# Sliding-window attention block with MLP on one core: Q and K as token rows transposed by DMA, V once per token, one-bank PSUM tiles

## The chip, the cores and the metric

The program runs on one core of a Trainium2 chip. The metric is the device time of the whole program in microseconds; three runs of the kernel before gave 184.72, 181.6 and 182.56 us, median 182.56 us. Engine names are those of the profile: PE is TensorE (PEld its weight loads), DVE is VectorE, ACT is ScalarE, POOL is GpSimd, and SP is SyncE, the queue from which nearly every DMA is issued. L12 is line 12 of the kernel file that is spoken of.

## What is computed

One transformer block on 2048 tokens of width 448 (16 heads of 28), all tensors bf16. A vector `c` gives six modulation rows. Attention is local and dilated: each token looks at itself and the 7 tokens at distance 2, 4, ... 14 before it.

```python
sa, ca, ga, sb, cb, gb = split(silu(c) @ w_mod, 6)
h = layernorm(x) * (1 + ca) + sa
q, k, v = heads(h @ wqkv)                       # 16 heads of 28
logits = q[s] . k[s - 2*w] * 28**-0.5           # w = 0..7, masked where s - 2*w < 0
x = x + ga * (softmax(logits) @ v) @ wo
h = layernorm(x) * (1 + cb) + sb
x = x + gb * (gelu(layernorm(h) @ w1 + b1) @ w2 + b2)     # 448 -> 1792 -> 448
```

## The kernel before, in words

**Layout.** The tokens are split by parity `s` (the dilation is 2, so a window is 8 neighbours of one parity) and into eight blocks `jb` of 2 x 128 tokens. The list of steps in `ORDER` (L32) is the program: each name is a method of the class, and each engine runs its instructions in the order in which the list issues them. `SLOTS` (L68) gives each step its buffer. Nothing is reordered later.

**Norm and transpose.** `s1`, `r1` and `n1` normalise a block. Blocks 0 to 3 are transposed on PE (`tr`, L385) and moved out of PSUM with the modulation applied (`ev`, L392, half on DVE and half on ACT). Blocks 4 to 7 are transposed by DMA from SP (`dT`, L402) and then modulated on DVE (`sc`, L407). The result is `hT`, channels on partitions, with 16 columns of zeros ahead.

**Q and K.** Each of the 16 heads is padded from 28 to 32 columns: `wc` (L441) spreads the weights, and `qk` (L448) computes four pieces of 256 padded channels, with weights stationary and tokens moving, for the groups of blocks 0, 1, 2+3, 4+5, 6+7. The result has channels on partitions, as the logits need it, and `qe` (L467) copies it to `qT` and `kT` on ACT. A piece is an accumulation in two halves, `first` (L415, eight matmuls) and `second` (L422, six matmuls): pairs of 64-row matmuls share the array, and the second half swaps the row halves. Between the halves stands `ob` (L432), a nop on SP, ACT, POOL or DVE that waits for the first half; the second half waits for the nop. So a nop that stands in a queue behind something slow holds PE up.

**V and the attention step.** The attention runs in nine steps `i` of 2 x 57 queries per parity. `v_` (L480) computes V anew for the 64 keys of each of the four windows of a step, 28 matmuls of 64 x 64 x 448 per step, and `ve` (L503) copies it on ACT. `L` (L512) makes the logits, 64 matmuls of 57 columns; `eA` and `eB` (L526) exponentiate them on ACT; `mA` and `mB` (L537) mask them on DVE; `AV` (L548) makes the sums and the outputs; `ln` (L567) and `rx` (L571) make 1/sum on ACT; `mu` (L575) multiplies on DVE. `wo` (L583) and `x1` (L591) project and add the residual.

**The MLP.** `s2` to `n3` norm and modulate, `dY` (L627) transposes by DMA, `f1` (L631, again in halves), `ge` (L652) and `f2` (L656) run over four chunks of 512 tokens, `fo` (L663) adds and `dS` stores. The last three attention steps lie among the MLP's first two chunks.

**PSUM.** Four tiles of two banks each (L97). One ACT or DVE instruction empties both banks: 896 to 1024 columns for Q, K, V, the logits, the sums, `x1` and most of `fo`.

**The row broadcast.** `rowm` (L301) makes four modulation rows on PE, `rowc` copies them, `dR` (L313) writes them to DRAM, and `dR2` (L316) reads them back to all partitions. Both are issued on SP, and `dR2` waits for `dR`.

Of the kernel before, what the change touches and what calls it, by code (L numbers as in the profile page):

```python
# [36 lines left out]
qA.0.1 ob.POOL.q.0.0 ob.ACT.q.1.2 n1.2 r1.3 qB.0.0 ob.ACT.q.0.1 qB.1.2 qe.0.0 tr.2 n1.3 qe.1.2 rowm ev.2.3 ev.2.2
ev.2.0 ev.2.1 tr.3 rowc qB.0.1 ev.3.2 ev.3.1 qA.0.2 ev.3.0 ev.3.3 s1.6 qA.1.1 ob.SP.q.0.2 qe.0.1 qB.0.2 ob.SP.q.1.1
qA.2.2 qe.0.2 dR s1.5 r1.6 qB.1.1 ob.SP.q.2.2 L.0 qe.1.1 s1.4 r1.5 qB.2.2 eA.0 dB qA.2.1 eB.0 mA.0 r1.4 qA.1.0 s1.7
ob.SP.q.2.1 qe.2.2 qB.2.1 ob.SP.q.1.0 qB.1.0 qe.2.1 qA.2.0 mB.0 r1.7 n1.4 dR2 qe.1.0 AV.0 ob.POOL.q.2.0 n1.5 dT.4  # L40
n1.6 qB.2.0 ln.0 qA.1.3 rx.0 dT.6 b1T ob.DVE.q.1.3 b1c qB.1.3 qe.2.0 mu.0 vA.1 dT.5 qe.1.3 vA.2 ob.POOL.v.1 wos vB.1
# [20 lines left out]
r2.7 n2.7 h2.7 f2.3.1 s3.7 r3.7 f2.5.0 n3.7 fo.3 dY.7 xp.6 dS.3 f2.5.1 fA.3.0 fo.5 fA.3.1 ob.SP.f.3.0 xp.7 dS.5
fB.3.0 ob.SP.f.3.1 fB.3.1 ge.3.0 fA.3.2 ge.3.1 ge.3.3 fA.3.3 ob.SP.f.3.2 ge.3.2 fB.3.2 ob.SP.f.3.3 fA.3.4 ge.3.5
ge.3.4 fB.3.3 ob.SP.f.3.4 fA.3.5 ge.3.6 ge.3.7 fB.3.4 ob.SP.f.3.5 fA.3.6 ge.3.9 ge.3.8 fB.3.5 ob.SP.f.3.6 fB.3.6
ge.3.11 f2.4.1 ge.3.10 ge.3.12 ge.3.13 f2.6.0 fo.4 dS.4 f2.6.1 f2.7.0 fo.6 dS.6 f2.7.1 fo.7.0 dS.7.0 fo.7.1 dS.7.1
"""
# [675 lines left out]
```

## Time and profile before

| | before |
|---|---|
| median of three runs | 182.56 us (181.6 to 184.72) |
| the profiled execution: span from the first to the last instruction | 182.2 us (the page gives no other time of it) |
| PE busy | 170.8 us, 2538 matmuls |
| DVE, ACT, POOL busy | 112.5, 105.0, 43.3 us |
| DMA | 15.51 MB, 21455 packets |
| mean granted TensorE clock | 0.958 |

The page gives busy time by engine, then 40 equal slices of the span (4.56 us each) in tenths of busy time, then the chain of work that ended last and the costliest groups. A group of the costliest instructions reads: line, engine, operation, output <- input, shape, count | busy us, mean ns of one | idle time before it and what ended it. A row of the windows table gives busy time, with the number of instructions in brackets, in one stretch of the span.

### The profile page before, as it was taken

What the parts mean: (1) busy time and instruction counts of PE and PEld (TensorE: products, weight loads), DVE (VectorE), ACT (ScalarE), POOL (GpSimd) and SP (SyncE); (2) the same over time, 40 slices, a digit from 0 to 9 for tenths busy, and PEclk for the clock granted to TensorE, in tenths of its full rate; (3) what the DMA queues carried; (4) which work ended last, traced back from release to release, by engine and by line L of the source; (5) the groups of instructions that cost most, each with busy time, mean ns of one, the idle gap of its engine ahead of it and who ended that gap; (6) DMA issues with size and microseconds to landing.
All of it is one profiled execution on the core that took longest, in us unless ns stands there. A gap on an engine that the chain in (4) does not pass through costs nothing.

```text
span 182.2 us, 5815 instructions
## 1 busy us (share of the span) xinstructions
PE 170.8 (94%) x2538; PEld 86.3 (47%) x2539; DVE 112.5 (62%) x264; ACT 105.0 (58%) x145; POOL 43.3 (24%) x77
## 2 busy tenths in 40 slices
PE   7999679979999979999999999999999999999990
PEld 2556335634444453444454554554544554454550
DVE  5858757599969789589788604785970772002022
ACT  3177619777967497487884879650887000585000
POOL 7404062000050442062402500224520224400000
PEclk9969969999999995899999999999999999999998
DMA  5999994997000300300080130013103004100111
GB/s 150 321 393 302 375 312 101 117 255 153 4 4 2 61 4 4 63 0 5 0 105 14 56 58 4 4 24 84 54 4 58 0 0 108 54 0 0 54 50 50
DMA packets 21455, 15.51 MB, mean 85 GB/s; under 512 B 13301, under 2 KB 20982, under 8 KB 21430
## 3 DMA queue, kind: packets, MB, share of 16 engines
q1 hardware_dynamic: 21428, 15.14, 32.1%
q8 instruction: 20, 0.33, 0.8%
q14 instruction: 5, 0.04, 0.1%
q10 hardware_dynamic: 2, 0.00, 0.0%
HBM read 10.04 MB, written 1.95 MB: 66 GB/s over the span
## 4 chain that ended last, share of the span: by engine, by line
PE 74%; DMA 8%; DVE 7%; ACT 4%; issue 2%; SPq 1%; POOL 1%; DVEq 0%
PE P L660 21%; PE P L419 18%; PE P L428 13%; PE P L588 7%; PE P L489 7%; DMA rowd<-zt 3%; DMA bc<-rowd 3%; DMA yT<-in_w_mod_dram 2%; PE P L563 2%; DVE st L348 2%; PE P L522 1%; PE P L554 1%; PE P L261 1%; PE P L292 1%; ACT et L527 1%
## 5 line engine op out<-in xcount | busy, mean ns | idle before, releaser
L653 ACT ACTIVATE hm<-P,b1c 128x512 bf16<-128x512 f32 x56 | 34.1, 691 | 22.4 <-PE P L428 22.3
L660 PE MATMUL P<-w2s,hm 128*128 128x448 bf16 x224 | 43.4, 353 | 0.0
L660 PEld LDWEIGHTS <-hm 128*128 128x128 bf16 x224 | 21.6, 98 | 20.6 <-issue 0.8
L419 PE MATMUL P<-yT,w1s 64*128 64x512 bf16 x224 | 27.1, 376 | 0.2 <-DVE x L665 0.2
L597 POOL TENSOR_TENSOR xp<-x,gbb 128x896 f32<-128x896 bf16 x8 | 15.2, 1897 | 40.2 <-DVE x L593 27.7
L665 DVE TENSOR_TENSOR x<-P,xp 128x896 bf16<-128x896 f32 (+1 forms) x9 | 8.8, 985 | 25.8 <-PE P L660 25.7
L354 POOL TENSOR_SCALAR rs<-mv 128x2 f32<-128x2 f32 x22 | 6.7, 303 | 70.8 <-DVE mv L350 61.8
L428 PE MATMUL P<-yT,w1s 64*128 64x512 bf16 x168 | 20.9, 376 | 0.0
L348 DVE BATCH_NORM_STATS2 st<-x 128x6 f32<-128x448 bf16 x32 | 18.3, 615 | 0.9 <-DMA x<-in_A_x_dram 0.5
L489 PE MATMUL P<-wv,hT 64*64 64x448 bf16 x252 | 17.5, 397 | 0.4 <-SPq L437 0.2
L593 DVE TENSOR_TENSOR x<-P,x 128x896 bf16<-128x896 f32 x8 | 8.7, 1090 | 14.5 <-PE P L588 14.5
L419 PEld LDWEIGHTS <-w1s 64*128 64x128 bf16 x224 | 11.1, 94 | 13.0 <-issue 1.2
L527 ACT ACTIVATE et<-P 128x912 bf16<-128x912 f32 x18 | 16.1, 942 | 1.7 <-PE P L522 1.7
L419 PE MATMUL P<-hT,wqk 64*128 64x512 bf16 (+1 forms) x160 | 16.9, 347 | 0.1
L428 PE MATMUL P<-hT,wqk 64*128 64x512 bf16 (+1 forms) x120 | 13.6, 349 | 3.6 <-SPq L437 3.6
L355 POOL TENSOR_TENSOR rs<-rs,nhalf 128x2 f32<-128x2 f32 x22 | 16.0, 726 | 1.8
L568 ACT ACTIVATE rc<-P 128x912 f32<-128x912 f32 x9 | 8.5, 942 | 10.4 <-PE P L554 10.4
L540 DVE TENSOR_TENSOR et<-et,mask 128x912 bf16<-128x912 bf16 x18 | 11.3, 652 | 4.5 <-ACT et L527 4.4
L588 PE MATMUL P<-wo,qT 128*128 128x448 bf16 x64 | 13.5, 353 | 0.1
L428 PEld LDWEIGHTS <-w1s 64*128 64x128 bf16 x168 | 8.8, 94 | 9.4
L578 DVE TENSOR_TENSOR qT<-P,rc 128x456 bf16<-128x456 f32 x18 | 10.5, 624 | 2.9 <-ACT rc L573 2.9
L509 ACT CAST vs<-P 128x896 bf16<-128x896 f32 x9 | 8.1, 907 | 6.2 <-PE P L489 6.2
(79 smaller groups left out, 187.2 us busy)
## 6 DMA issues: line engine op xcount, KB each, us to landing
w1s<-in_B_w_dram SPq DMA_DIRECT2D x4, 448.0 KB, 11.7
w2s<-in_B_w_dram SPq DMA_DIRECT2D x2, 784.0 KB, 15.6
out_dram<-x SPq DMA_DIRECT2D x7, 224.0 KB, 2.3
hm<-in_w_mod_dram SPq DMA_DIRECT2D x1, 1344.0 KB
hm<-in_A_wqkv_dram SPq DMA_DIRECT2D x4, 224.0 KB, 5.1
x<-in_A_x_dram SPq DMA_DIRECT2D x1, 896.0 KB
yT<-in_w_mod_dram SPq DMA_DIRECT2D x3, 224.0 KB, 4.1
x<-in_A_x_dram SPq DMA_DIRECT2D x2, 224.0 KB
```

Source lines behind the costliest of these rows:

```text
L348: nc.vector.bn_stats(out=self.st[:, b + s, :], in_=src[:, s, :])
L355: nc.gpsimd.tensor_tensor(out=r, in0=r, in1=self.nhalf[:], op=ALU.pow)
L419: mm = self.nc.tensor.matmul(outs[t], lhsT=lhs(t, r, kt), rhs=rhs(t, r, kt), start=(kt == 0), stop=False)
L428: mm = self.nc.tensor.matmul(outs[o], lhsT=lhs(o, r, kt), rhs=rhs(o, r, kt), start=False, stop=(n == 2))
L489: mm = self.nc.tensor.matmul(t[64 * s:64 * s + 64, o, 0:D], lhsT=self.hT[r, s, kt, k0:k0 + NK], rhs=self.wv[r, kt, :], start=(part == 0 an ...
L527: self.nc.scalar.activation(out=self.et[:, self.sl(f"e{i}"), 2 * h:2 * h + 2, :], in_=self.ps(f"L{'AB'[h]}{i}")[:, :, 0:8 * NQ], func=ACT.Exp,
L540: self.nc.vector.tensor_tensor(out=e, in0=e, in1=m, op=ALU.mult)
L578: self.nc.vector.tensor_tensor(out=self.qT[:, s, :, c0:c0 + SW], in0=self.ps(f"O{i}")[:, s, 0:8 * NQ].rearrange("p (m c) -> p m c", m=4), ...
L588: self.nc.tensor.matmul(p[:, s, 0:D], lhsT=self.qT[:, s, m, c0:c0 + 128], rhs=self.wo[:, m, :], start=(m == 0), stop=(m == 3))
L597: self.nc.gpsimd.tensor_tensor(out=self.xp[:, self.sl(f"xp{jb}"), :, :], in0=self.x[:, jb, :, :], in1=self.gbb2[:].unsqueeze(1).to_broadca ...
L653: self.nc.scalar.activation(out=self.hid(c)[:, ft, :], in_=self.ps(f"F{c}.{ft // 2}")[:, ft % 2, :], func=ACT.Gelu_apprx_tanh, bias=self.b ...
L660: self.nc.tensor.matmul(p[:, s, 0:D], lhsT=h[:, ft, 128 * b:128 * b + 128], rhs=self.w2s[:, ft, :], start=(ft == 0), stop=(ft == FT - 1))
```

## The change

- **Q and K with tokens as rows.** `qk` takes the token block as the stationary operand (128 tokens) and the weights, unpadded, as the moving one: 448 columns of Q into one bank and 448 of K into another, for each block and parity. `wc` is gone; the weights are used as they come from DRAM. Each bank is copied to a staging tile `qks` with the heads spread to 32 columns (`qe`, on ACT or DVE, one bank each), and a DMA transpose from SP (`qT`) turns the 128 x 1024 staging tile into the transposed layout `qkT`. There are 16 such transposes.
- **V once per token.** `v` is computed as Q and K are, 14 matmuls per block. `ve` copies it to `vst`, `vw` writes it to a scratch tensor `vd` in DRAM, and `vr` reads the overlapping windows back, two per step. `dZ` writes the zero rows at the ends.
- **PSUM** is eight tiles of one bank, and every instruction that empties PSUM works on one bank: `ex`, `ln`, `rx`, `mu`, `x1`, `fo`.
- **Transposes of h.** Blocks 2 to 7 by DMA; only blocks 0 and 1 on PE. `sc` is one instruction per piece, on DVE or ACT.
- The modulation columns (`mod`) are made one slab of weights at a time, `wqk` and `wv` share the memory of the hidden layer, and `ORDER` and `SLOTS` are new throughout. The rest of the MLP's arithmetic is as before.

```diff
-        self.P = [ps.tile([128, 2, 512], FP32, name=f"P{i}") for i in range(4)]
+        self.P = [ps.tile([128, 512], FP32, name=f"P{i}") for i in range(8)]
...
-            return self.wqk[r, kt, 128 * (2 * p + o):128 * (2 * p + o) + 128]
+            return self.hT[r, s, kt, 128 * jb:128 * jb + 128]
...
-            return self.hT[r, :, kt, c0:c0 + 128 * nj]
-        return [t[:, 0, 0:n], t[:, 1, 0:n]], lhs, rhs
+            return self.wqk[r, kt, D * o:D * o + D]
+        return [p[:, 0:D] for p in self.ps(f"Q{jb}_{s}")], lhs, rhs
...
+    def qe(self, eng, jb, s, o):
+        out = self.qks[:, self.sl(f"q{jb}_{s}"), o, :].rearrange("p (h e) -> p h e", e=32)[:, :, 0:DH]
+        self.copy(eng, out, self.ps(f"Q{jb}_{s}")[o][:, 0:D].rearrange("p (h e) -> p h e", e=DH))
+
+    def qT(self, jb, s):
+        c0 = PADL + 128 * jb
+        src = self.qks[:, self.sl(f"q{jb}_{s}"), :, :].rearrange("p o n -> p (o n)")
+        self.nc.sync.dma_start_transpose(out=self.qkT[:, s, :, c0:c0 + 128], in_=src)
+
+    def v(self, jb):
+        def lhs(o, r, kt):
+            return self.hT[r, o, kt, 128 * jb:128 * jb + 128]
+
+        def rhs(o, r, kt):
+            return self.wv[r, kt, :]
+        return [p[:, 0:D] for p in self.ps(f"V{jb}")], lhs, rhs
+
+    def vw(self, jb):
+        a = WIN - 1 + 128 * jb
+        self.nc.sync.dma_start(out=self.vd[:, a:a + 128, :].rearrange("s r d -> r s d"),
+                               in_=self.vst[:, self.sl(f"vw{jb}"), :, :])
+
+    def vr(self, i, s):
+        src = self.vd[s, SW * i:SW * i + NK, :]
+        src = bass.AP(src.tensor, src.offset, [list(src.ap[0]), [NQ * D, 2], [1, D]])
+        self.nc.sync.dma_start(out=self.vs[64 * s:64 * s + 64, self.sl(f"v{i}"), :, 0:D], in_=src)
...
-        self.nc.scalar.activation(out=self.et[:, self.sl(f"e{i}"), 2 * h:2 * h + 2, :],
-                                  in_=self.ps(f"L{'AB'[h]}{i}")[:, :, 0:8 * NQ], func=ACT.Exp,
+    def ex(self, i, r):
+        self.nc.scalar.activation(out=self.et[:, self.sl(f"e{i}"), r, :], in_=self.ps(f"L{i}")[r][:, 0:8 * NQ],
...
-            if jb < 4:
+            if jb < NTR:
...
+NACT = 2
+NTR = 2
```

Three places of the new order matter to the prediction. The first is the start of ACT's queue, with what each instruction waits for (hT<-P is `ev`, hT<-hT is `sc`; DMAHW names the semaphore of a DMA; wqk<-hm is `wc`). Before:

```order
L400 ACTIVATE hT<-P_65,mcol 128x2x128 x2
L446 COPY wqk<-hm 128x512 x2
L400 ACTIVATE hT<-P_66,mcol 128x2x128 x2
L446 COPY wqk<-hm 128x512
L509 CAST vs<-P_64 128x2x448
L478 CAST kT<-P_63 128x2x2x128
```

The change, up to the first copy of Q and the first of V:

```order
L416 ACTIVATE hT<-P_65,mcol 128x2x128 [waits DVE_49,PE_49]
L416 ACTIVATE hT<-P_67,mcol 128x2x128 [waits DVE_49,PE_49]
L416 ACTIVATE hT<-hT,mcol 128x2x128 [waits DMAHW5_49]
L416 ACTIVATE hT<-hT,mcol 128x2x128
L475 CAST qks<-P_68 128x16x28 [waits PE_49]
L475 CAST qks<-P_70 128x16x28 [waits PE_49]
L475 CAST vst<-P_63 128x448 [waits PE_49]
```

The weight copies are gone, and two `sc` of block 2, which wait for that block's DMA transpose, now stand ahead of the first copy of Q; the nop `ob.A.Q0_0`, for which the second half of the first Q and K piece waits on PE, stands in this queue right behind them.

The second place is ACT from the last copies of Q and K ahead of the first logits (`L.0`) on. Before:

```order
L478 CAST qT<-P_65 128x2x2x128
L527 ACTIVATE et<-P_64 128x912
L527 ACTIVATE et<-P_63 128x912
L478 CAST kT<-P_66 128x2x2x256
L478 CAST qT<-P_65 128x2x2x256
L478 CAST qT<-P_64 128x2x2x128
L568 ACTIVATE rc<-P_65 128x912
L573 ACTIVATE rc<-rc 128x912
```

The change:

```order
L475 CAST qks<-P_70 128x16x28
L531 ACTIVATE et<-P_67 128x456
L531 ACTIVATE et<-P_66 128x456
L531 ACTIVATE et<-P_63 128x456
L531 ACTIVATE et<-P_65 128x456
L475 CAST qks<-P_68 128x16x28
L475 CAST qks<-P_69 128x16x28
L475 CAST qks<-P_64 128x16x28
L475 CAST vst<-P_67 128x448
L475 CAST vst<-P_66 128x448
```

One step's exponentials were two instructions of 912 columns and are four of 456; the first `ln` moved back behind the exponentials of two more steps.

The third place is SP around the row broadcast (rowd is `dR`, bc is `dR2`). Before:

```order
L187 DMA wo<-in_A_wo_dram 28x4x448 x4
L314 DMA rowd<-zt 128x448
L191 DMA b1r<-in_B_b_dram 14x128
L192 DMA b2bc<-in_B_b_dram 128x448
L318 DMA bc<-rowd 128x4x448
L405 DMA_TRANSPOSE hT<-yz 128x8x128 x3
```

The change:

```order
L424 DMA_TRANSPOSE hT<-yz 128x8x128
L512 DMA vs<-vd 64x2x448
L332 DMA rowd<-rows 128x448
L484 DMA_TRANSPOSE qkT<-qks 128x8x128
L206 DMA wo<-in_A_wo_dram 28x4x448
L336 DMA bc<-rowd 128x4x448
L484 DMA_TRANSPOSE qkT<-qks 128x8x128
L512 DMA vs<-vd 64x2x448
```

SP now also issues the transposes of Q and K and the reads of V, and the second transpose of block 3 stands behind `dR2`.

More of the change, by code (lines that the diff above doesn't have):

```diff
@@ L37 @@
[L37 to L41, printed above, removed]
@@ L62 @@
[L62 to L65, printed above, removed]
+i.mask i.z i.eps warm.3.4 i.one dX.0.1 dC cT warm.0.5 s1.0 silu0 silu1 warm.2.4 i.maskc r1.0 n1.0 i.ones dM.0 dX.2.2
@@ L288, in mod, with silu2 @@
+    def silu2(self):
+        self.nc.vector.tensor_copy(out=self.silub[:], in_=self.silu[:].unsqueeze(2).to_broadcast([128, 4, 32]))
+    def mod(self, kt):
+        p, r = self.ps("mod"), slice(0, min(128, D - 128 * kt))
         for v in range(2):
             for j in range(4):
-                for kt in range(4):
-                    r = slice(0, min(128, D - 128 * kt))
-                    self.nc.tensor.matmul(p[:, 1, 4 * v + j:4 * v + j + 1],
-                                          lhsT=self.wm1[r, kt, v * D + KO[j]:v * D + KO[j] + 128],
-                                          rhs=self.silu[r, kt:kt + 1], start=(kt == 0), stop=(kt == 3))
+                n = 8 * kt + 4 * v + j
+                self.nc.tensor.matmul(p[:, n:n + 1], lhsT=self.wm1[r, kt, v * D + KO[j]:v * D + KO[j] + 128],
+                                      rhs=self.silu[r, kt:kt + 1], start=True, stop=True)
@@ L310, in rowc @@
     def rowc(self):
-        self.nc.scalar.copy(out=self.rows, in_=self.ps("R")[:, 0, 0:D])
+        self.nc.scalar.copy(out=self.rows[:], in_=self.ps("R")[:, 0:D])
     def dR(self):
-        self.nc.sync.dma_start(out=self.rowd[:], in_=self.rows)
+        self.nc.sync.dma_start(out=self.rowd[:], in_=self.rows[:])
     def dR2(self):
@@ L478, in qe @@
             self.nc.scalar.copy(out=out, in_=src)
-    def v_(self, i, part):
-        t = self.ps(f"V{i}")
-        for n in range(4 if part == 0 else 3):
-            for row in range(2):
-                o = row if part == 0 else 1 - row
-                kt = n if part == 0 else REST[o][n]
-                k0 = PADL + SW * i + NQ * o - (WIN - 1)
-                r = slice(64 * row, 64 * row + 64)
-                for s in range(2):
-                    mm = self.nc.tensor.matmul(t[64 * s:64 * s + 64, o, 0:D], lhsT=self.hT[r, s, kt, k0:k0 + NK],
-                                               rhs=self.wv[r, kt, :], start=(part == 0 and n == 0),
-                                               stop=(part == 1 and n == 2), tile_position=(64 * row, 64 * s))
-                    if part == 1 and n == 0:
-                        self.tc.add_manual_dep(mm.ins, self.half[f"V{i}"], SYNC, reason="half")
-        if part == 0:
-            self.half[f"V{i}"] = mm
@@ L640, in rhs @@
             return y[r, :, kt, :]
-        return [t[:, 0, :], t[:, 1, :]], lhs, rhs
+        return [t[:, :] for t in self.ps(f"F{c}_{p}")], lhs, rhs
     def fA(self, c, p):
-        self.first(f"F{c}.{p}", *self.f1(c, p))
+        self.first(f"F{c}_{p}", *self.f1(c, p))
     def fB(self, c, p):
-        self.second(f"F{c}.{p}", *self.f1(c, p))
+        self.second(f"F{c}_{p}", *self.f1(c, p))
     def hid(self, c):
@@ L681, in emit @@
             name, args = "i_" + args[0], []
-        name = {"silu": "silu_", "w2s": "w2s_", "b1c": "b1c_", "wo": "wo_", "xp": "xp_"}.get(name, name)
-        getattr(self, name)(*[int(a) for a in args])
-WC_DVE = {(0, 0), (0, 2), (1, 0), (1, 2)}
-QE_DVE = set()
-VE_DVE = set()
+        name = {"w2s": "w2s_", "b1c": "b1c_", "wo": "wo_", "xp": "xp_"}.get(name, name)
+        getattr(self, name)(*[int(a) if a.isdigit() else a for a in args])
+NACT = 2
+NTR = 2
 @with_exitstack
```

347 lines of the change are left out of this document (162 added, 185 removed).

## The prediction, made before the changed kernel ran

> **What bounds the kernel now.** I read the page first, then the table of windows cut where the work changes its kind, then the chain, the groups and the queue of SP.
>
> ```profile
> span 182.2 us, 5815 instructions
> PE 170.8 (94%) x2538; PEld 86.3 (47%) x2539; DVE 112.5 (62%) x264; ACT 105.0 (58%) x145; POOL 43.3 (24%) x77
> ...
> GB/s 150 321 393 302 375 312 101 117 255 153 4 4 2 61 4 4 63 0 5 0 105 14 56 58 4 4 24 84 54 4 58 0 0 108 54 0 0 54 50 50
> ```
>
> PE is busy 94% of the span. The windows (us, then busy time of PE, PEld, DVE, ACT and POOL, granted clock, DMA share, GB/s) are cut at the first logits (26.9), the first matmul of the MLP's first chunk (79.5), that of its third chunk (128.5) and the last matmul (178.1); the stretches are A (from the start to 26.9; its second half is shown), B, C, D and the tail.
>
> ```profile
> 12.80:26.90 14.10, 11.42 (x153) 6.59 (x152) 9.97 (x30) 7.55 (x14) 4.78 (x10) 0.86 1.06 339
> 26.90:79.50 52.60, 49.82 (x1237) 25.00 (x1237) 41.83 (x97) 39.80 (x46) 11.10 (x14) 0.94 0.36 68
> 79.50:128.50 49.00, 48.71 (x743) 24.95 (x744) 33.52 (x71) 32.88 (x45) 13.63 (x19) 1.00 0.18 36
> 128.50:178.10 49.60, 49.57 (x344) 24.01 (x340) 17.51 (x36) 19.73 (x31) 8.18 (x11) 1.00 0.11 32
> 178.10:182.20 4.10, 0.00 (x0) 0.00 (x0) 1.16 (x2) 0.00 (x0) 0.00 (x0) 0.79 0.16 56
> ```
>
> The reader is to see that B, C and D are PE's: 49.8 of 52.6, 48.7 of 49.0, 49.6 of 49.6 us. But in B DVE (41.8) and ACT (39.8) stand not far behind. A change that takes work from PE and gives it to these two can win at most the distance between them.
>
> **PE's part, from the chain** (start, us, what), where matmuls run back to back at the full clock:
>
> ```profile
> 9.14 0.55 PE P L390 x8
> ...
> 15.61 1.31 PE P L419 x24
> ...
> 44.89 1.29 PE P L428 x12
> ...
> 47.05 0.63 PE P L522 x64
> ...
> 51.68 0.32 PE P L554 x8
> 51.99 0.55 PE P L563 x64
> ...
> 56.50 1.62 PE P L588 x8
> ...
> 76.36 0.69 PE P L489 x12
> ...
> 113.66 2.76 PE P L660 x14
> ```
>
> A 512-column matmul of Q and K costs 1.29/12 = 0.1075 us, one of 256 columns 1.31/24 = 0.0546. Before, Q and K are 168 of the first and 112 of the second, 24.2 us. After, 224 of 448 columns; at 0.1075 x 448/512 = 0.094 each, 21.1 us. V before is 252 x 0.69/12 = 14.5 us; after 112 x 0.094 = 10.5 us. Sixteen of 32 PE transposes go, 16 x 0.55/8 = 1.1 us. PE loses 8.2 us in all; were PE the bound throughout, the span would be 174.0 us.
>
> **What ACT and DVE gain.**
>
> ```profile
> L653 ACT ACTIVATE hm<-P,b1c 128x512 bf16<-128x512 f32 x56 | 34.1, 691 | 22.4 <-PE P L428 22.3
> L348 DVE BATCH_NORM_STATS2 st<-x 128x6 f32<-128x448 bf16 x32 | 18.3, 615 | 0.9 <-DMA x<-in_A_x_dram 0.5
> L527 ACT ACTIVATE et<-P 128x912 bf16<-128x912 f32 x18 | 16.1, 942 | 1.7 <-PE P L522 1.7
> L540 DVE TENSOR_TENSOR et<-et,mask 128x912 bf16<-128x912 bf16 x18 | 11.3, 652 | 4.5 <-ACT et L527 4.4
> L478 ACT CAST kT<-P 128x1024 bf16<-128x1024 f32 x6 | 6.0, 1013 | 2.6 <-PE P L428 2.6
> L478 ACT CAST kT<-P 128x512 bf16<-128x512 f32 x4 | 2.4, 591 | 2.1 <-PE P L428 2.1
> L358 DVE TENSOR_SCALAR zz<-x,mv,rs 128x448 bf16<-128x448 bf16 x24 | 8.5, 395 | 3.3 <-POOL rs L355 3.2
> L350 DVE BATCH_NORM_AGGREGATE mv<-st 128x2 f32<-128x6 f32 x48 | 7.2, 174 | 0.0
> L411 DVE TENSOR_SCALAR hT<-hT,mcol 128x256 bf16<-128x256 bf16 x16 | 4.4, 341 | 0.2 <-DMA hT<-yz 0.2
> L400 ACT ACTIVATE hT<-P,mcol 128x256 bf16<-128x256 bf16 x8 | 4.4, 567 | 3.1 <-DVE hT L397 2.8 <-PE P L390 0.3
> L665 DVE TENSOR_TENSOR x<-P,xp 128x448 bf16<-128x448 f32 x2 | 1.2, 620 | 4.2 <-PE P L660 4.2
> L311 ACT CAST zt<-P 128x448 bf16<-128x448 f32 x1 | 0.5, 522 | 0.0
> ```
>
> From the two casts of 1024 and 512 columns, a column costs 0.825 ns on ACT and an instruction about 170 ns beside. So an instruction of half the width is not half the price: an exponential of 456 columns is 942 - 456 x 0.825 = 566 ns, and a copy of 448 columns 522 ns (the row at L311). Run back to back the instructions overlap a little (16.1 us busy for 18 x 0.942 = 17.0, or 95%).
>
> Count B again as the new order has it, from the first logits to the first matmul of the MLP: eight steps of logits, six `AV`, four `wo`, Q and K and V of blocks 2 to 7, and the row matmuls.
> - PE: 8 x 0.63 + 6 x 0.87 + 4 x 1.62 + 168 x 0.094 + 84 x 0.094 + 1.2 = 41.7 us (was 49.8).
> - ACT: 32 exponentials x 0.566, 23 `ln` and `rx` x 0.57, 29 copies x 0.522, 8 `sc` x 0.567 make 50.9, times 0.95 = 48.3 us (was 39.8).
> - DVE: 12 masks x 0.63, 19 `mu` and `x1` x 0.61, 9 copies out of PSUM, 10 `sc` x 0.275 (4.4/16), 8 pairs of normalisations x 0.72, 7 statistics x 1.44, and 8 small or full-width operations, some 5. A copy out of PSUM on DVE is in no row; it is bounded by 0.275 (the `sc`, out of SBUF) and 0.62 (the L665 row, out of PSUM), and I take 0.6, since both read fp32 from PSUM: 48 us (was 41.8).
>
> No engine has more than 48.3 us, but three have over 41 and they feed each other. Lower bound of B: ACT as dense as PE was, 48.3 x 52.6/49.8 = 51.0. Upper bound: cut B at the third and the seventh logits; the largest engine's sums are 9.6 (DVE), 33 (ACT) and 11.8 (DVE), and with the pieces between single logits each at its largest engine 59.5; so far up it goes if no slack is carried over. I take **54.5**, nearer to the lower bound, since a queue can run behind by one step.
>
> **A.** Before, the first logits come at 26.9. After, the last copies of block 0 and the two transposes decide. DVE's queue must go through four statistics and the first three normalisations ahead of the modulation columns:
>
> ```profile
> 2.76 0.48 DVE L243 COPY mask<-m 128x912 bf16<-128x912 bf16 x1
> ...
> 5.98 0.16 DVE L283 TENSOR_TENSOR silu_c<-P,e_c 128x4 bf16<-128x4 f32 x1
> ```
>
> The silu is done at 6.1; a mask 0.48, two `n1` of 0.72 and two statistics of 1.44 make 10.9, when the transpose of block 2 can be issued. What such transposes took (ns on SP, min/median/max, and us to landing), what a plain DMA held SP for, and what nops on SP cost PE (us in total, times, longest):
>
> ```profile
> L629 SPq DMA_TRANSPOSE yT<-yz x8: 1232/1232/1977, 61.0 to 149.8; - x8
> ...
> DMA to landing us min/median/max: 2.7/3.1/4.5
> ```
>
> ```profile
> 24.00 0.37 SPq L314 DMA_DIRECT2D rowd<-zt  x1
> ```
>
> ```profile
> L405 SPq DMA_TRANSPOSE hT<-yz x4: 1302/1546/2950, 31.8 to 38.8; - x4
> ```
>
> ```profile
> PE P L428 <- SPq L437: 3.6, 2, 2.5
> ```
>
> It lands 3.1 to 4.5 us later, at about 14.9; two `sc` of 0.57 on ACT follow, then the nop, PE's two second halves (12 x 0.094), two copies (0.52 and 0.6), and two transposes from SP, each holding SP for 1.23 to 1.55 us, the second landing 3.1 us after its issue: 16.0 + 1.1 + 1.1 + 1.4 + 3.1 = 22.7. With the other blocks' matmuls in between I take **23.3** (21.5 to 25).
>
> **C.** PE has 13 pairs of `f1` (1.505 each), four `f2`, four `wo`, one step of logits and three `AV`: 40.1 us (was 48.7). DVE comes to 39.5 by the same prices: 7 statistics 10.1, 8 pairs of normalisations 5.8, 16 `mu`, `x1` and `fo` 9.8, and 22 full-width operations on bf16 (masks, `h2`, the scaling of w2) at the mask's 0.63, 13.9. ACT has 26 gelus at 34.1/56 = 0.61 and 17 half-width instructions, 25 us without its table loads. DVE at 98% of PE cannot follow without waits; between 40.3 and 45 I take **42.5**. **D** holds more than before, 15 pairs and 12 `f2`: 22.6 + 32.4 = 55.0, and DVE and ACT have room, so **55.2**. The **tail** ends with the same add and store: **4.1**.
>
> Sum: 23.3 + 54.5 + 42.5 + 55.2 + 4.1 = 179.6 us of span, against 182.2. The median of the runs stands 0.4 above the profiled span, so **180.0 us** against 182.56. PE's 8.2 us go mostly into waits on ACT and DVE.
>
> **Rivals.**
>
> *The three engines overlap almost fully.* The queues carry slack over, and ACT in B is as dense as PE was. Then A 22.3, B 51.0, C 41.0: 22.3 + 51.0 + 41.0 + 55.0 + 4.1 = 173.4, with 0.4 **173.8 us**. For it speaks that the eight one-bank tiles set each bank free on its own; against it that the longest sum in B changes from DVE to ACT and back.
>
> *SP and the DMA engines decide.* In B, SP issues 19 transposes (1.23 to 1.55) and 28 other DMAs (some 0.4 each): 35 to 41 us. One transpose also fills the 16 engines for 0.88 x 2.0 = 1.8 us (the window at 62 below), 34 us for 19, and 5.7 MB of other traffic at 393 GB/s is 15 us. The queue is in order, and five of PE's nops for Q and K stand in it, one right ahead of the first logits and four behind. In the trace of before two such nops cost PE 3.6 us, 1.8 each. At that price five cost 9.0 us, B is 63.5, and the time **189 us**, slower. It decides from where SP's issues and waits together pass 54.5 us. Against it: most nops now stand on POOL and ACT. The Trainium skill (DMA: Bandwidth & Descriptors, section "Issuing engines are not separate DMA queues") calls the time to issue a DMA usually small relative to the DMA; by it this rival would fall away. The 1.23 us of a landing of 3.1 say otherwise here.
>
> *The clock falls more often.* A view of PE by windows (us, busy, clock, DMA share, GB/s):
>
> ```profile
> 62.00:64.00 2.00, 1.75 (x64) 1.00 0.88 131
> 64.00:68.00 4.00, 2.67 (x199) 0.98 0.02 4
> 68.00:74.00 6.00, 5.86 (x146) 0.50 0.01 3
> ```
>
> After 4 us in which PE worked 2.7 us on small matmuls, it ran at half clock for 6 us. In the new B, PE has 41.7 us for 54.5. If 10 us more of its work in B and C run at half clock, that costs up to 5 us: **185 us**. The Trainium skill (TensorE: Matmul & The Clock Gate, section "Why this matters for your kernels") asks only that no idle gap be longer than about 3 us; by that rule PE's short gaps cost nothing and this rival falls away. The rows show the fall without a gap of that length, so I keep it.
>
> **How the numbers follow.** Forecast 0.45 (own range 176 to 184), full overlap 0.22, SP 0.22, clock 0.11. The range takes in the first rival and the second: 172.5 to 189.5; the lowest ends of all terms together make 172, the highest 190. A difference of 2%, 3.65 us, is about what a measurement of this kernel can tell from none: faster means below 178.9. That is the whole first rival and 0.18 of the forecast, 0.40; slower, above 186.2, is most of the second rival and a little of the third, 0.22; the rest is 0.38.
>
> **What would show it.** Right: matmuls of 448 columns at 0.094 us; PE's busy time down by about 8 us, but its share in B down to some 77%; ACT and DVE near 48 us each in B; half-width exponentials at 0.57 us; the last matmul 55 us after the first of the third chunk. Wrong: a B of over 60 us with PE waiting on SP's nops or on `qkT`; a B at 51 with ACT without gaps; or long stretches of half clock.

## The result, and the profile after

The changed kernel takes **191.34 us** (four executions, 190.0 to 193.37), the kernel before 182.88 us beside it (181.6 to 184.72). The ratio is **1.042, 95% interval 1.033 to 1.052**: slower. 180.0 us was forecast, with a range up to 189.5. Some executions, here and below, took over 1.5% longer than the fastest of their kernel; the ratios leave them out and the medians do not, and without them the median is 190.55 us here, 184.57 for `e3_v_windows` and 177.52 for `e13_no_qk_t`, and one execution of 188.96 us is left of `e2_v_pool`.

The page of the changed kernel, its span, busy times and DMA:

```profile
span 188.3 us, 5539 instructions
PE 165.0 (88%) x2327; PEld 79.7 (42%) x2328; DVE 116.4 (62%) x281; ACT 101.4 (54%) x190; POOL 43.2 (23%) x73
...
DMA packets 45274, 24.13 MB, mean 128 GB/s; under 512 B 32750, under 2 KB 44801, under 8 KB 45249
...
q1 hardware_dynamic: 45220, 23.76, 58.8%
```

and the page of the kernel before, the same two lines of its DMA:

```profile
DMA packets 21455, 15.51 MB, mean 85 GB/s; under 512 B 13301, under 2 KB 20982, under 8 KB 21430
...
q1 hardware_dynamic: 21428, 15.14, 32.1%
```

PE works 5.8 us less, as the change intends, but the span is 6.1 us longer. The packets have doubled, 19,449 of the 23,819 new ones are under 512 bytes, and the time they take went from 32% to 59% of the 16 engines' span.

The table of windows, cut as in the prediction at the first logits (22.2), the first matmul of the MLP (86.4), that of its third chunk (129.8) and the last matmul (184.7):

```profile
0.00:22.20 22.20, 16.87 (x154) 8.05 (x155) 16.86 (x56) 8.78 (x19) 8.26 (x27) 1.00 0.94 237
22.20:86.40 64.20, 51.77 (x1247) 25.73 (x1245) 42.56 (x100) 42.53 (x91) 7.22 (x16) 0.89 1.05 201
86.40:129.80 43.40, 41.41 (x564) 19.51 (x554) 37.51 (x88) 30.68 (x50) 13.62 (x19) 1.00 0.37 82
129.80:184.70 54.90, 54.90 (x379) 26.42 (x378) 18.89 (x38) 19.42 (x31) 14.12 (x12) 1.00 0.14 42
184.70:188.30 3.60, 0.01 (x1) 0.00 (x0) 0.62 (x1) 0.00 (x0) 0.00 (x0) 1.00 0.11 37
```

| stretch | before | forecast | after |
|---|---|---|---|
| A, to the first logits | 26.9 | 23.3 | 22.2 |
| B, to the MLP | 52.6 | 54.5 | **64.2** |
| C, to the third chunk | 49.0 | 42.5 | 43.4 |
| D, to the last matmul | 49.6 | 55.2 | 54.9 |
| tail | 4.1 | 4.1 | 3.6 |

The whole miss is in B. There the DMA share is 1.05 (0.36 before), and no compute engine is full: PE 81%, ACT and DVE 66% each. What the engines wait for (us in total, times, longest):

```profile
PEld L526 <- DMA qkT<-qks: 8.5, 5, 3.6
ACT qks L475 <- DMA qkT<-qks: 8.0, 2, 4.4
...
PE P L526 <- DMA qkT<-qks: 7.1, 3, 3.1
...
PE P L445 <- SPq L453: 3.8, 2, 2.8
```

PE waits at the logits (L526) for Q and K to land in `qkT`, and ACT waits for a staging tile `qks` that a transpose has not yet read. The chain in order of time shows three of these landings at full length:

```profile
45.79 5.77 DMA qkT<-qks
51.56 0.04 issue
51.60 0.70 PE P L526 x64
...
59.70 5.33 DMA qkT<-qks
...
73.14 5.98 DMA qkT<-qks
```

5.3 to 6.0 us from issue to landing; I had taken 3.1 to 4.5, and only in A. The clock falls behind such a wait. Windows of 2 us around the first of them (us, busy time of PE, PEld, DVE, ACT and POOL, granted clock, DMA share, GB/s):

```profile
48.00:50.00 2.00, 0.49 (x6) 0.05 (x2) 0.35 (x1) 0.04 (x1) 0.00 (x0) 1.00 1.10 173
50.00:52.00 2.00, 0.40 (x52) 0.39 (x52) 0.00 (x0) 0.34 (x1) 0.00 (x0) 1.00 1.18 233
52.00:54.00 2.00, 2.00 (x40) 0.73 (x33) 1.20 (x3) 2.00 (x6) 0.00 (x0) 0.61 1.20 292
54.00:56.00 2.00, 2.00 (x7) 0.76 (x5) 2.00 (x5) 1.32 (x3) 0.00 (x0) 0.54 0.83 217
```

PE stands nearly idle for 3 us, then runs at about half clock: (0.39 + 0.46) x 2.00 = 1.7 us are lost. B's mean clock of 0.89 stands for four such falls, 0.11 x 64.2 = 7 us.

So there were two suspects in B, the transposes' landings and the clock, and behind the landings three possible causes: the rate of the DMA engines, SP's time to issue, or the three staging tiles. A fourth is the mixed order of ACT, DVE and PE.

### The profile page after: what moved, and what is told of

Same layout as the page of the kernel before. It is cut to its first block, busy times and chain, and to the rows that moved or that the text cites. A ratio compares the mean times of both kernels' runs of the same rounds, so it can differ in the third digit from the quotient of the medians.

```text
span 188.3 us, 5539 instructions
## 1 busy us (share of the span) xinstructions
PE 165.0 (88%) x2327; PEld 79.7 (42%) x2328; DVE 116.4 (62%) x281; ACT 101.4 (54%) x190; POOL 43.2 (23%) x73
## 4 chain that ended last, share of the span: by engine, by line
PE 61%; DMA 14%; DVE 9%; ACT 6%; SPq 5%; issue 2%; ACTq 0%; POOLq 0%; DVEq 0%
PE P L650 23%; PE P L436 15%; PE P L445 12%; DMA qkT<-qks 9%; PE P L578 7%; DVE st L367 3%; SPq L484 2%; DMA hm<-in_w_mod_dram 2%; ACT et L531 2%; PE P L526 2%; SPq L424 1%; DMA rowd<-rows 1%; ACT hm L643 1%; ACT qks L475 1%; DVE zz L377 1%
## 5 line engine op out<-in xcount | busy, mean ns | idle before, releaser
L654 DVE TENSOR_TENSOR x<-P,xp 128x448 bf16<-128x448 f32 x16 | 9.6, 618 | 30.6 <-PE P L650 30.6
L436 PE MATMUL P<-hm,hT 64*128 64x448 bf16 x192 | 22.7, 376 | 1.3 <-ACT hT L416 1.3
L531 ACT ACTIVATE et<-P 128x456 bf16<-128x456 f32 x36 | 17.0, 557 | 7.4 <-PE P L526 7.3
L445 PE MATMUL P<-hm,hT 64*128 64x448 bf16 x144 | 17.1, 359 | 4.1 <-SPq L453 3.8
L475 ACT CAST qks<-P 128x448 bf16<-128x448 f32 x25 | 12.4, 542 | 12.9 <-DMA qkT<-qks 8.0
L578 PE MATMUL P<-wo,qkT 128*128 128x448 bf16 x64 | 17.3, 425 | 0.0
L583 DVE TENSOR_TENSOR x<-P,x 128x448 bf16<-128x448 f32 x16 | 9.5, 618 | 8.7 <-PE P L578 8.7
L436 PEld LDWEIGHTS <-hT 64*128 64x128 bf16 x192 | 9.3, 99 | 10.8 <-issue 2.6
L526 PE MATMUL P<-qkT 28*64 28x57 bf16 x576 | 7.0, 203 | 7.1 <-DMA qkT<-qks 7.1
L559 ACT ACTIVATE rc<-P 128x456 f32<-128x456 f32 x18 | 9.1, 558 | 7.1 <-PE P L545 7.1
L568 DVE TENSOR_TENSOR qkT<-P,rc 128x456 bf16<-128x456 f32 x18 | 10.9, 627 | 1.9 <-ACT rc L564 0.8
```

The source lines that it names most:

```text
L436: mm = self.nc.tensor.matmul(outs[t], lhsT=lhs(t, r, kt), rhs=rhs(t, r, kt), start=(kt == 0), stop=False)
L445: mm = self.nc.tensor.matmul(outs[o], lhsT=lhs(o, r, kt), rhs=rhs(o, r, kt), start=False, stop=(n == 2))
L475: self.nc.scalar.copy(out=out, in_=src)
L526: self.nc.tensor.matmul(dst, lhsT=self.qkT[rr, s, 4 + m, k0:k0 + NK], rhs=self.qkT[rr, s, m, q0:q0 + NQ], start=True, stop=True, tile_posi ...
L531: self.nc.scalar.activation(out=self.et[:, self.sl(f"e{i}"), r, :], in_=self.ps(f"L{i}")[r][:, 0:8 * NQ], func=ACT.Exp, scale=float(DH) ** ...
L568: self.nc.vector.tensor_tensor(out=self.qkT[:, s, 0:4, c0:c0 + SW], in0=self.ps(f"O{i}")[s][:, 0:8 * NQ].rearrange("p (m c) -> p m c", m=4 ...
```

## The experiments

**1. Transfers by themselves** (`e4_dma_alone`). None of the computation; six transfers a phase, each phase after the one before has landed, `tr` a transpose of 128x1024, `vw` a store of 224 KB, `vr` a read of 112 KB:

```python
for n in range(6): tr(n)
...
for n in range(6): vw(n, nc.sync)
...
for n in range(6): tr(n); vw(n, nc.sync); vr(n, nc.sync)
...
for n in range(6): tr(n); vw(n, nc.gpsimd); vr(n, nc.gpsimd)
```

> Only transfers, none of the reference's computation; the output is the input x. In turn, each phase after the one before has landed: 6 V reads; 6 transposes of 128x1024; 6 V stores of 224 KB; 6 V reads of 112 KB; 6 triples of transpose, store, read, all issued by SP; the same triples with store and read issued by POOL. Theory (DMA engines): transposes back to back are over 1.4 us apart and fill the engines (share over 0.9); a triple takes the sum of the three alone, with either issuer. Rival 1 (SP's issue): transposes are 1.25 us apart with the engines partly idle; a triple from SP takes the sum of the issue times (1.25 + 0.45 + 0.5 = 2.2 us), and with POOL's help 1.25.

SP's queue, start and length of the issues, of the transposes alone, the first triple from SP, and the transposes of the last phase, whose stores and reads POOL issued:

```profile
24.47 8.23 SPq L53 DMA_TRANSPOSE dst<-src  x6
...
57.95 1.26 SPq L53 DMA_TRANSPOSE dst<-src  x1
59.26 0.58 SPq L56 DMA_DIRECT2D vd<-vst  x1
59.88 0.59 SPq L62 DMA_DIRECT2D vs<-ve  x1
60.52 1.32 SPq L53 DMA_TRANSPOSE dst<-src  x1
...
80.34 16.47 SPq L53 DMA_TRANSPOSE dst<-src  x6
```

Alone a transpose goes out every 8.23/6 = 1.37 us, and it fills the engines: the window of that phase, its last landing included, has a DMA share of 0.85, so 0.85 x 9.60/6 = 1.36 us of all 16 engines for each (busy time of DVE and POOL, then clock, DMA share, GB/s):

```profile
24.40:34.00 9.60, 0.04 (x2) 0.00 (x0) 1.00 0.85 164
```

A triple from SP takes 60.52 - 57.95 = 2.57 us. With POOL issuing two of the three, SP needs 16.47/6 = 2.75 us for each transpose, although it has nothing else to do: the issue itself is held up. The windows of the two phases of triples:

```profile
57.90:75.00 17.10, 0.02 (x1) 0.00 (x0) 1.00 0.91 209
80.30:97.00 16.70, 0.01 (x1) 7.22 (x11) 1.00 1.06 182
```

The engines are full or nearly so either way (0.91 and 1.06), and the triple costs no less when another engine issues part of it. That speaks against SP's issue as a cause of its own. It does not exclude it: POOL's transfers run in another queue of this profile (`q0`, software_dynamic), so the two phases differ in more than the issuer. (The Trainium skill, in DMA: Bandwidth & Descriptors, section "Issuing engines are not separate DMA queues", says that DMAs share the same 16 engines, whichever engine starts them. What it adds there, that the time to issue is usually small, doesn't hold for these issues of 2.75 us.)

**2. V's round trip** (`e1_no_v`, `e2_v_pool`, `e3_v_windows`). Left out, issued by POOL, and undone:

```diff
 # e1_no_v: vw and vr
-        self.nc.sync.dma_start(out=self.vd[:, a:a + 128, :]...
+        return
 # e2_v_pool: vw and vr
-        self.nc.sync.dma_start(...)
+        self.nc.gpsimd.dma_start(...)
 # e3_v_windows: as in the kernel before, into five tiles vs
+                    self.nc.tensor.matmul(t[o][64 * s:64 * s + 64, 0:D], lhsT=self.hT[r, s, kt, k0:k0 + NK], ...
+        self.copy(eng, self.vs[:, self.sl(f"v{i}"), o, 0:D], self.ps(f"V{i}")[o][:, 0:D])
```

> The changed kernel without V's way through the scratch tensor: the 8 stores and 18 reads are left out, attention reads zeros for V; the computation of V and its copies stay. Theory (DMA engines): the DMA share of 1.06 in the stretch from the first logits (22.2) to the first matmul of the MLP (83.0) means that 16 transposes and V's traffic fill the DMA engines; with V's 3.8 MB gone the transposes land in 3 to 4 us instead of 4.7, PE's wait of 7.1 us on qkT and ACT's of 8.0 us on the staging tile at least halve: 182 to 186 us. Rival 1 (SP's issue): SP was without a gap from 20 to 57 us; 26 issues of 0.4 to 0.6 us, some 13 us, go: also 182 to 186. Rival 2 (mixed work of ACT and DVE, clock): the work of PE, ACT and DVE is the same: 189 to 192.

> The changed kernel with V's 8 stores and 18 reads issued by POOL instead of SP, same bytes and same places in the order. Theory (DMA engines): the traffic is the same, so the transposes still land 4.5 us or more after their issue: 188 to 192 us. Rival 1 (SP's issue): SP is rid of some 13 us of issues and of its waits on V's stores: 182 to 186 us, as without V. Rival 2: 189 to 192. A lower and an equal time tell rival 1 from the theory; POOL's own time to issue may add a wait for its nops and for rs.

> One part undone: V by windows as in the kernel before (9 times, 252 matmuls instead of 224 halves, copied straight to the tile that attention reads), Q, K, the one-bank tiles and the rest as in the changed kernel. The output is the reference's. Theory and rival 1: PE gains 4 us of work, DMA loses V's 26 transfers; the stretch from the first logits to the MLP comes down by 4 to 8 us: 184 to 188 us. Rival 2: PE has 4 us more and nothing else is better: 192 to 195 us.

Without V's traffic: 188.75 us, ratio to before 1.032 (1.022 to 1.042). That is 2.6 us less than the changed kernel by the medians, with intervals of the two ratios that overlap, and short of the 182 to 186 that I and SP's rival expected. Issued by POOL: 192.54 us (188.96 to 193.27); no execution came to the 182 to 186 of SP's rival, so SP's time to issue V's transfers is not the cause. V by windows: 186.32 us (184.3 to 189.03), in the range expected, although PE has 4 us more to do. The windows of B of the first and the third:

```profile
24.50:85.40 60.90, 48.93 (x1247) 25.66 (x1245) 42.00 (x99) 42.73 (x93) 7.30 (x16) 0.92 0.93 159
```

```profile
22.70:78.60 55.90, 48.22 (x1333) 24.27 (x1333) 42.15 (x99) 42.79 (x93) 7.72 (x16) 0.97 0.98 173
```

Both are without V's transfers, and yet the DMA share stays at 0.93 and 0.98 and B above 54.5, so V's round trip is not the whole miss. How much of it is V's, these two don't settle: B is 3.3 us shorter with the transfers left out and 8.3 us shorter with V by windows. Part of that difference stands in one place, the matmuls of logits 3, of the first run and then of the third:

```profile
52.30 0.79 PE L525 MATMUL P<-qkT 28*64 28x57 bf16 x64 [3.61 <-DMA qkT<-qks]
```

```profile
47.61 0.70 PE L519 MATMUL P<-qkT 28*64 28x57 bf16 x64 [1.59 <-DMA qkT<-qks]
```

The transpose that they wait for took 8.3 us from issue to landing in the first run and 6.3 us in the third, and PE waited 3.6 and 1.6 us for it. Leaving V's transfers out did not bring this landing forward; why it came later is not shown. (The first run also zeroes the whole of `vs` on POOL. Its first logits come at 24.5 us; in `e5_fill` below, whose start is that of the changed kernel, they come at 25.1, both with a clock of 0.86 in A, so the zeroing isn't shown to cost anything.)

**3. The clock** (`e5_fill`, `e8_before_fill`). Matmuls on zeros, which nobody needs, where PE waits:

```diff
+    def fill(self, b, n):
+        for _ in range(n):
+            self.nc.tensor.matmul(self.P[b][:, :], lhsT=self.zt[:, 0:128], rhs=self.zt[:], start=True, stop=True)
 # in ORDER of the changed kernel
- qB.3.0 ... L.3 ... L.5 ... L.6
+ fill.5.12 qB.3.0 ... fill.6.14 L.3 ... fill.0.10 L.5 ... fill.4.12 L.6
 # in ORDER of the kernel before
- qB.0.2 ... L.5 ... AV.3
+ fill.3.12 qB.0.2 ... fill.0.3 L.5 ... fill.0.5 AV.3
```

> The changed kernel with 48 more matmuls of 512 columns on zeros, written to a free PSUM bank, right ahead of the four places where PE stood idle for 1.7 to 3.1 us (12 ahead of the second half of Q and K of block 3, 14, 10 and 12 ahead of logits 3, 5 and 6): 10 us of work that no one needs. Theory (gaps pull down the clock): in the changed kernel's trace each of the four gaps is followed by some 3.4 us of granted clock 0.5, 1.7 us lost each; with the gaps filled the falls are gone: 183 to 186 us although PE does more. Rival (only the landing counts): the logits wait as long as before and the clock falls for another reason: 190 to 194 us.

> The kernel before with 20 more matmuls of 512 columns on zeros: 12 ahead of the second half of Q and K that waited 2.5 us at 21.3 us, 3 ahead of logits 5 and 5 ahead of the third AV (65 to 67 us). Theory (gaps pull down the clock): the falls at 23 to 27 us and 67 to 75 us, 5.1 us in all, go in part: 178 to 181 us. Rival: no change or the added work shows: 182.5 to 185 us.

The changed kernel so filled: 189.41 us, ratio 1.031 (1.023 to 1.038). By the medians that is 2 us less with 10 us more work; the intervals of the ratios overlap. B of that run:

```profile
25.10:88.50 63.40, 55.92 (x1291) 28.40 (x1294) 44.17 (x108) 44.03 (x94) 7.68 (x16) 1.00 1.09 203
```

The clock is 1.00 throughout and B is still 63.4 us. So the gaps do pull the clock down in this kernel, as I said, but what the falls cost is mostly waited for anyway, and my 6.8 us were wrong. The kernel before, filled, had a clock of 1.00 over its whole span in the profiled execution (0.976 to 0.991 in the others) and took 182.92 us, ratio 1.000 (0.995 to 1.004), not the 178 to 181 expected. There the added matmuls take PE some 20 x 10.8/44 = 4.9 us themselves (an estimate: the trace of the filled changed kernel has 44 of its 48 with 10.8 us), about the 5.1 us that the falls were to give back, so that run doesn't tell a gain paid back from no gain.

**4. Order and staging** (`e6_reorder`, `e7_stage8`).

```diff
 # e6_reorder, in ORDER
-qT.4.0 L.3 ex.3.1 ex.3.0 vw.4 wos.1 ... wo.0
+qT.4.0 vw.4 wos.1 ... wo.0 L.3 ex.3.1 ex.3.0
-L.5 ... wo.1 ... qA.6.0 AV.3
+wo.1 qA.6.0 L.5 ... AV.3
-L.6 ... wo.2
+wo.2 ... L.6
 # e7_stage8: five more tiles qks in the space of w2s, q0_0 ... q7_1 take the eight in turn
+        self.qb = [self.qks[:, k] for k in range(3)] + [self.w2s[:]... for k in range(5)]
```

> The changed kernel with logits 3, 5 and 6 and their exponentials moved behind work that stood right after them on PE: logits 3 behind wo of block 0, logits 5 behind wo of block 1 and the first half of Q and K of block 6, logits 6 behind wo of block 2. Theory (PE idles for the landing of transposes, and the clock falls after it): the waits of 3.1, 1.7 and 2.3 us are covered by 1.6 us of wo each, and falls of the clock of 1.7 us go: 182 to 187 us. Rival (the chain of copies, transposes and exponentials sets the pace, PE only waits elsewhere): 189 to 192 us.

> The changed kernel with 8 staging tiles for Q and K instead of 3 (five of them in the space of w2, which is loaded later). Theory A (the three staging tiles hold ACT): ACT's 8.0 us and DVE's 3.0 us of waits for a transpose to leave its staging tile go, copies come earlier: 185 to 188 us. Theory B (the transposes' own rate and landing decide): the copies come earlier, the transposes queue up instead and land as late: 190 to 192 us.

The new order is slower still, outside both ranges: 194.82 us, ratio 1.058 (1.051 to 1.066). Its chain shows a new wait:

```profile
50.06 4.18 DMA wo<-in_A_wo_dram
54.37 0.63 DVE wo L346
55.05 3.17 PE P L578 x8
```

`wo` of block 0, put ahead of logits 3, waits for its own weights, which take 4.18 us on the chain. The work that I thought ready wasn't. With eight staging tiles the time is 191.27 us, ratio 1.043 (1.035 to 1.050), unchanged as theory B had it. ACT no longer waits for a staging tile, but PE waits as before:

```profile
PE P L531 <- DMA qkT<-w2s: 6.6, 3, 3.0
```

**5. The transposes of Q and K** (`e9_half_t`, `e13_no_qk_t`, `e14_no_qk_t_windows`). Half of them left out, all of them, and all of them with V by windows:

```diff
 # e9_half_t
 def qT(self, jb, s):
+        if s == 1:
+            return
-   lhsT=self.qkT[rr, s, 4 + m, k0:k0 + NK], rhs=self.qkT[rr, s, m, q0:q0 + NQ]
+   lhsT=self.qkT[rr, 0, 4 + m, k0:k0 + NK], rhs=self.qkT[rr, 0, m, q0:q0 + NQ]
 # e13_no_qk_t, e14_no_qk_t_windows: the copies go to qkT themselves, qT does nothing
-        out = self.qks[:, self.sl(f"q{jb}_{s}"), o, :]...
+        out = self.qkT[:, s, 4 * o:4 * o + 4, c0:c0 + 112]
```

> The changed kernel with only the even tokens' Q and K transposed: 8 of the 16 transposes of Q and K are left out, the logits of the odd tokens read the even tokens' Q and K instead (same matmuls); all copies, stores, loads and the rest stay. Theory (the landing of the transposes is the chain of this stretch): logits wait for one transpose instead of two, 3 to 4 us after its issue instead of 5.3 to 6.0, at four to six steps, and falls of the clock go with it; from the first logits to the MLP 54 to 58 us instead of 64.2: 180 to 185 us. Rival (ACT and DVE, 42.5 us each in that stretch, and their mixed order set the pace): 188 to 191 us.

> The changed kernel without any of the 16 transposes of Q and K: the same 32 copies put Q and K straight, untransposed, where the logits read them, so the logits are of the wrong numbers but of the same size; V's round trip and the six transposes of h stay. Theory (the transposes' landings are the miss): the stretch from the first logits to the MLP falls from 64.2 to 52 to 56 us, near the forecast 54.5 that took a landing of 3.1 us: 180 to 183 us. Rival (V's round trip or the mixed work): it stays at 58 us or more, what half of the transposes left out gave: 184 us or more.

> As the run before, and V by windows instead of the round trip; logits of the wrong numbers, the same size. PE has 4 us more than the changed kernel. Theory: with no new transfer left the stretch is at the work of PE, ACT and DVE, 49 to 53 us: 176 to 180 us. Rival (mixed work of the new order): 56 us or more in the stretch, as with V by windows alone (55.9): 184 us or more.

Half left out: **184.45 us**, ratio 1.002 (0.999 to 1.006). All left out: **179.12 us**, ratio 0.980 (0.971 to 0.989). All, with V by windows: **177.36 us**, ratio 0.968 (0.962 to 0.974). B in the three, in this order:

```profile
23.90:81.50 57.60, 47.04 (x1249) 25.21 (x1248) 42.30 (x99) 42.81 (x94) 7.52 (x16) 0.97 0.95 183
```

```profile
23.20:73.60 50.40, 44.97 (x1247) 24.11 (x1246) 42.41 (x103) 42.50 (x94) 7.68 (x16) 1.00 0.69 165
```

```profile
24.00:71.30 47.30, 46.18 (x1331) 23.54 (x1329) 41.82 (x100) 42.52 (x93) 7.49 (x16) 1.00 0.50 109
```

B goes from 64.2 to 57.6 to 50.4: 6.6 us for eight transposes, 7.2 for the other eight, 13.8/16 = 0.86 us each (13 of the 16 are issued in B), with the work of PE, ACT and DVE the same. The clock returns to 1.00 by itself. The last two came out at or below what the theory expected. This settles it for the transposes as a whole. It also settles that the mixed order of the compute engines is no cause: left to themselves they do B in 50.4 us, and in 47.3 without V's reads and stores, though PE has 4 us more.

The two new uses of the DMA have no prices that add up. With V by windows the transposes cost B 55.9 - 47.3 = 8.6 us instead of 13.8. V's round trip costs B 64.2 - 55.9 = 8.3 us beside the transposes and 50.4 - 47.3 = 3.1 us without them. So each makes the other dearer, and 0.86 us is the price of a transpose beside V's transfers only.

**6. What stands ahead of a transpose** (`e10_w1_late`, `e11_windows_w1_late`). The four loads of w1 behind the last transpose, in the changed kernel and in `e3_v_windows`:

```diff
- ... dW1.0.0 ... dW1.0.1 ... dW1.1.1 ... dW1.1.0 ... qT.7.1 L.7
+ ... qT.7.1 dW1.0.0 dW1.0.1 dW1.1.0 dW1.1.1 L.7
```

> The changed kernel with the four loads of w1 (448 KB each) issued behind the last transpose of Q and K instead of between them at 57.8, 63.3, 69.9 and 71.7 us. Theory (plain loads ahead of a transpose in the same engines delay its landing): each load is some 1.3 us of the engines (448 KB at 340 GB/s); the waits of 5.3 and 6.0 us ahead of logits 5 and 6 come down to some 4 us: 186 to 189 us. Rival (transposes delay each other): 189.5 to 192 us, and the first matmul of the MLP may wait for w1.

> V by windows and w1 loaded late together, the output is the reference's: 182 to 185 us if both act by the theory (186.3 with V by windows alone, less up to 3 us from two landings); 185 to 188 if the loads of w1 don't matter.

Both missed: 193.77 us, ratio 1.052 (1.045 to 1.059), and 192.50 us, ratio 1.037 (1.026 to 1.048). The chain of `e10_w1_late`:

```profile
62.15 4.15 DMA qkT<-qks
...
72.80 4.88 DMA qkT<-qks
...
84.09 4.94 DMA vs<-vd
```

The two landings came down as expected, from 5.33 to 4.15 and from 5.98 to 4.88 us: one load of 448 KB ahead of the first and two ahead of the second had cost 1.2 and 1.1 us. The landing ahead of logits 3, with no such load before it in either order, stayed (5.77 and 5.93 us). But V's read behind the loads and a transpose `yT` now lands after 4.9 us and holds the last work ahead of the MLP. In `e11_windows_w1_late`, which has no such read, the first matmul of the MLP waits for its own transpose behind the loads:

```profile
82.40 3.60 PE L431 MATMUL P<-yT,w1s 64*128 64x512 bf16 x16 [5.59 <-DMA yT<-yz]
```

What two landings gained, a later one lost.

**7. Without any new transfer** (`e12_no_new_dma`, `e15_no_new_dma_warm`). Q and K computed already transposed, V by windows, everything else as changed; then ten matmuls on zeros more among the modulation:

```diff
-                mm = ... lhsT=self.hT[r, s, kt, 128 * jb:128 * jb + 128], rhs=self.wqk[r, kt, D * o:D * o + D]
+                mm = ... lhsT=self.wqk[r, kt, 128 * (4 * s + 2 * n + o):...+ 128], rhs=self.hT[r, :, kt, c0:c0 + 128]
- mod.0 mod.1 ... mod.2 ... mod.3
+ mod.0 warm.0.6 mod.1 ... warm.0.2 mod.2 ... warm.0.2 mod.3
```

> Both new uses of the DMA undone, the rest kept: V by windows, and Q and K computed already transposed (weights as the stationary operand padded to 32 columns a head as in the kernel before, 256 tokens' columns a matmul, two matmuls on zeros to open each bank), copied straight to qkT; the new order, one-bank tiles, the later loads and the six blocks transposed by DMA stay. The output is the reference's. PE has some 11 us more than the changed kernel (16 x 1.75 us of Q and K against 16 x 1.32, V 14.5 against 10.5). Theory (transposes' landings cost the changed kernel the time): no logits wait on a transpose, the stretch from the first logits to the MLP is at PE's or ACT's work, 50 to 54 us instead of 64.2 although PE does more: 178 to 184 us. Rival (the new order or the one-bank tiles cost it): 188 us or more.

> The version without both new uses of the DMA, whose output is the reference's, and 10 more matmuls on zeros among the small matmuls of the modulation, where PE stood idle for 1.6, 0.25 and 0.27 us at 7.5 to 10.5 us before the clock was 0.5 for ten us. If the gap causes the half clock, the first logits come at some 23 us instead of 27.5: 183 to 185 us. If not: 187 to 188.

187.49 us, ratio 1.020 (1.009 to 1.032), 3.5 us over what I expected; with the filling 184.74 us, ratio 1.008 (1.004 to 1.013), as expected. A and B of the first, then A of the second:

```profile
0.00:27.50 27.50, 23.42 (x247) 13.40 (x247) 18.39 (x62) 10.52 (x23) 8.23 (x29) 0.81 0.76 220
27.50:81.50 54.00, 51.30 (x1523) 33.06 (x1521) 41.86 (x97) 43.72 (x93) 7.49 (x16) 1.00 0.42 87
```

```profile
0.00:25.20 25.20, 22.19 (x256) 12.13 (x257) 17.48 (x59) 10.51 (x23) 8.23 (x29) 1.00 0.95 230
```

B is 54.0 us, 10 less than in the changed kernel, although PE's own work is more (51.3 us busy at full clock, against 45.0 with the transposes left out): the theory holds there. The time went into A, where the first logits come at 27.5 us; 2.3 us of it are the half clock from 10 to 20 us, which the filling removes. Of the 3.0 us that A is still longer than in the changed kernel, the copies that pad the weights stand with 1.4 us in the second run's chain; the rest is not shown. No version that computes the reference was faster than the kernel before.

## Why the prediction was wrong, and where it was right

**The step that failed is B, "I take 54.5".** The sum counted the work of PE, ACT and DVE and nothing of the DMA. The work was counted right or too high: without the transposes PE has 45.0 us in B (41.7 forecast), ACT 42.5 (48.3; the count of 92 instructions was right, but they overlap more than the 95% taken) and DVE 42.4 (48). The bounds of 51.0 and 59.5 priced how three engines feed each other; that costs at most the 5.4 us from PE's 45.0 to 50.4, and 1.1 us without V's transfers (PE 46.2 of 47.3). What belonged there is the way of Q and K: copy, issue, landing (5.3 to 6.0 us on the chain), logits, with 13 transposes of Q and K, six others and V's traffic in the same engines. It cost 64.2 - 50.4 = 13.8 us of B, and 191.34 - 179.12 = 12.2 us of the time; without V's traffic beside it, 8.6 us of B. The prediction had named the sign, a B of over 60 us with PE waiting on `qkT`.

**The landing was in my table, and I used it once**, in A, where 3.1 us were taken for the last transpose. A came out at 22.2 (23.3 forecast), but not by that way. The first logits did not wait for a landing (the second transpose, issued at 18.7, had landed by 22.2); the matmuls ahead of them waited for a nop on SP:

```profile
21.57 0.74 PE L445 MATMUL P<-hm,hT 64*128 64x448 bf16 x6 [1.04 <-SPq L453]
22.23 0.70 PE L526 MATMUL P<-qkT 28*64 28x57 bf16 x64
```

And with the same start A took 25.1 us in `e5_fill`. That the size came out is in part luck. In B, where each step of logits hangs on a landing, none was priced (the expectation of `e13_no_qk_t`, which says that 54.5 took one, is wrong there).

**A small term was mis-sized too:** the 0.4 us from span to time. It set the median of three executions against the span of another one. In the profiled execution of the changed kernel the time is 190.0 us and the span 188.3, 1.7 us apart.

**The rival of SP and the DMA engines** named the place and nearly the size (B 63.5, 189 us), not the mechanism. It priced SP's nops at 9.0 us; PE waited 3.8 us on them. Moving 26 issues to POOL did not bring the 182 to 186 us. What it had right is that transposes fill the engines; a transpose takes 1.37 us of them alone, not the 1.8 worked out from the window at 62. Its chance of 0.22 was too low, since its own sum (34 us for 19 transposes and 15 for the rest) already stood close to B's length.

**The rival of full overlap** came near by its number, B at 51.0 by its sum and 50.4 measured with the transposes gone. Its reason, ACT as dense as PE was, didn't hold: ACT had 42.5 of the 50.4 us. The transposes were what it left out.

**The rival of the clock** saw the falls and mis-sized them. There are four in B, each behind a wait. Filled up, B hardly changes (63.4); with the waits gone, the falls go too. They are mostly a consequence.

**Right:** a matmul of 448 columns at 1.14/12 = 0.095 us (0.094 forecast), in the chain; the half-width exponential and copy, in the groups:

```profile
14.66 1.14 PE P L445 x12
```

```profile
L531 ACT ACTIVATE et<-P 128x456 bf16<-128x456 f32 x36 | 17.0, 557 | 7.4 <-PE P L526 7.3
...
L475 ACT CAST qks<-P 128x448 bf16<-128x448 f32 x25 | 12.4, 542 | 12.9 <-DMA qkT<-qks 8.0
```

557 and 542 ns against 566 and 522. C (43.4 for 42.5), D (54.9 for 55.2) and the tail came out as forecast, so between the two profiled executions the change gains 26.9 + 49.0 + 49.6 + 4.1 - (22.2 + 43.4 + 54.9 + 3.6) = 5.5 us outside B. A varies by up to 2.9 us with the same start (22.2 and 25.1), so this sum is no more certain than that.

**Open:** how the 0.86 us of a transpose in B divides between the engines' time, the delay of a landing and SP's issue; leaving a transpose out takes away all three. A run that keeps one and drops the others wasn't tried. Nor is it shown why V by windows (B 55.9) is 5 us better than V's transfers simply left out (60.9), beyond the later landing ahead of logits 3.

## What to carry to other kernels

A tile that goes through a DMA transpose on its way to the next matmul is priced as a stage of the chain (here 5 to 6 us under load, 16 of them 12 us of the time beside V's transfers), and the sum for a stretch has a line for the DMA engines beside those for PE, ACT and DVE. When a DMA share near 1 stands beside compute engines at 66 to 81%, leaving out one kind of transfer at a time, and then both, told more here than moving or reordering them, since their prices didn't add up. A falling clock behind a wait was here first a sign of the wait: filling the gaps of the changed kernel raised the clock and left the length of B.
